# Block-diagonal q half by VectorE copies, residuals in the activation buffers, and a fixed VectorE order through the Out-projection

## The chip, the cores and the metric

The kernel runs on one core of one Trainium2 chip. The metric is the device time of one execution, in microseconds (us); 17 runs of the kernel before have a median of 1339.47 us. TensorE (PE in the profile) multiplies, VectorE (DVE) and ScalarE (ACT) work element by element, SyncE (SP) issues the transfers (DMA), and GpSimd (POOL) does next to nothing here. PEld is TensorE's weight load.

## The reference

Two layers, each an attention and a token-mixing MLP, on x of 2048 x 1024 in bf16. The attention has 32 heads of 32 columns; a position looks at eight positions, itself and every second one before it. The MLP mixes the 2048 positions, with 3584 hidden units. Both are added to x.

```python
def _A_ref(x, wqkv, wo):
    H = 32; Dh = D // H
    W, dil = 8, 2
    q, k, v = ...
    off = jnp.arange(W) * dil
    idx = pos[:, None] - off[None, :]
    logits = einsum("bhsd,bhswd->bhsw", q, kg) * Dh ** -0.5
    attn = softmax(where(idx >= 0, logits, -1e9))
    o = einsum("bhsw,bhswd->bhsd", attn, vg)
    return o.reshape(B, S, D) @ wo

def _B_ref(x, w1, b1, w2, b2):
    u = gelu(einsum("bsd,sf->bdf", layernorm(x), w1) + b1)
    return (einsum("bdf,fs->bds", u, w2) + b2).transpose(0, 2, 1)

x = x + _A_ref(layernorm(x), A_wqkv, A_wo)
x = x + _B_ref(layernorm(x), B_w1, B_b1, B_w2, B_b2)
x = x + _A_ref(layernorm(x), A_wqkv, A_wo)
x = x + _B_ref(layernorm(x), B_w1, B_b1, B_w2, B_b2)
```

## The kernel before, in words

The positions are split by their residue c modulo 2, which makes the dilated window a plain window of eight neighbours. A tile (c, i) is 128 such positions; there are 16. `order` lists them, c = 0 first.

A layer starts with the normalised x, transposed (`hT`), and the value projection. Then come 16 **units**: unit u is one group g of four heads (128 columns) and one residue c. A unit has two **visits** (b = 0, 1), each for four tiles. In a visit TensorE runs, in a fixed order (`in_order`): the scores of (u, b); the values of the visit before; two chunks of the q/k projection of the unit after (`qk_chunk`; visit 0 does the two halves of q, visit 1 those of k), eight matmuls each.

- `scores` (line 372) multiplies blocks of 32 keys with `qB`, in which q stands block-diagonally: head h fills partitions 32h to 32h+31 of column block h, all else is zero. So one matmul gives the scores of four heads. The last matmul of visit 0 reaches eight columns into the second half of q. ScalarE then takes the exponential (`pc`, line 384), and VectorE multiplies four pieces of 32 partitions with the band mask into `Pm` (line 389).
- `qk_chunk` (line 348): for q, ScalarE casts the product to `qs` (pool `qsp`, two buffers, line 360), and four transfers bring the heads' rows to their places in `qB` (line 363), all issued by SP, in order (`chain_("SP", ...)`). Two halves of four heads make eight transfers for a unit. For k a cast into `kT` is enough (line 357).
- `values` (line 393) multiplies `Pm` with the values and with ones into one accumulator `acc` (a single buffer); ScalarE turns the sums into reciprocals `rd` (lines 425 and 426), and VectorE multiplies them into `oT` (line 428), which frees `acc`.

In the last unit there is no next projection. Instead the two visits run the Out-projection of tiles (0, 0) to (0, 3), and the other twelve tiles follow. `out_proj` (line 447) does two halves of 512 columns, eight matmuls each (line 456). VectorE adds the residual `xr` to each (line 458, result `xn`), `xn` is stored, and the normalisation for the MLP follows at once: two statistics (line 181), their aggregate (183), two small ScalarE steps (175, 176), a small VectorE step (193), and ScalarE's activation into `h2` (194). `xr`, `xn` and `rd` share the six buffers of the pool `x2p`; two residuals are loaded ahead. The products use two `m` buffers, so that a half can start only when the add of the half before the last is done.

The MLP follows: `gemm1` (its first block takes the tiles of `h2` one after the other, line 488) and `gemm2` (line 531), whose tiles VectorE adds to the residual (line 534) and SP stores. The pool `gop` has 14 buffers. They hold the activations `g` in the MLP; in the attention eight of them hold `oT`, and six are free.

The order of work on VectorE, ScalarE and SP is set when the program is built, by a scheduler that keeps what `in_order` and `chain_` fix and puts the rest where it can go.

Of the kernel before, what the change touches and what calls it, by code (L numbers as in the profile page):

```python
# [9 lines left out]
ACT = mybir.ActivationFunctionType  # L10
# [4 lines left out]
P = 128  # L15
# [3 lines left out]
DIL = 2  # L19
# [6 lines left out]
def kernel(  # L26
# [42 lines left out]
    def pool(name, bufs, **kw):  # L69
        return ctx.enter_context(tc.tile_pool(name=name, bufs=bufs, **kw))  # L70
# [8 lines left out]
    pcp = pool("pcp", 2)  # L79
    qsp = pool("qsp", 2)  # L80
    dram = pool("dram", 1, space=bass.MemoryType.DRAM)
# [266 lines left out]
    def qk_chunk(u, wts, part, n):  # L348
        g, c = divmod(u, DIL)
        ps = m_tile()  # L350
        lo = c * SC + n * 512
        for kt in range(KD):
            mm = nc.tensor.matmul(ps[:], lhsT=wts[part][:, kt, (g % 2) * P:(g % 2 + 1) * P], rhs=hT[:, kt, lo:lo + 512],  # L353
                                  start=(kt == 0), stop=(kt == KD - 1))
        ls = slice(n * 512, (n + 1) * 512)
        if part:
            nc.scalar.copy(out=kT[u % 2][:, ls], in_=ps[:])  # L357
        else:
            qs = qsp.tile([P, 512], BF16, name="qs", tag="qs")
            nc.scalar.copy(out=qs[:], in_=ps[:])  # L360
            for h in range(HG):
                hp = slice(h * DH, (h + 1) * DH)
                chain_("SP", lambda: nc.sync.dma_start(out=qB[u % 2][hp, h, ls], in_=qs[hp, :]))  # L363
        return mm
# [7 lines left out]
    def scores(u, b):  # L372
# [3 lines left out]
        for i in range(HB):  # L376
            lo = (b * HB + i) * P
            for r in range(P // KG):
# [6 lines left out]
                             func=ACT.Exp, scale=scale, bias=shift[:])  # L385
        for r in range(P // KG):
            rp = slice(r * KG, (r + 1) * KG)
            mk = band[rp].unsqueeze(1).unsqueeze(1).to_broadcast([KG, HB, HG, GW])
            nc.vector.tensor_tensor(out=Pm[rp, :, s0:s0 + HB, r * KG:r * KG + GW].rearrange("p h t k -> p t h k"),  # L389
                                    in0=pc[rp], in1=mk, op=ALU.mult)  # L390
        return mm

    def values(u, b, v, oT):
# [33 lines left out]
        lo = c * SC + t0 * P  # L427
        nc.vector.tensor_tensor(out=oT[g][:, lo:lo + HB * P], in0=acc[:, 0, :], in1=rd[:], op=ALU.mult)
        return mm

    def load_wo(tiles):
# [10 lines left out]
    def load_xr(res):  # L442
        t = x2("xr")
        xrs.append(t)
        chain_("SP", lambda: nc.sync.dma_start(out=t[:], in_=res(*todo.pop(0))))

    def out_proj(c, i, oT, wo, res, dst, h2):
        xr = xrs.pop(0)
        if todo:
            load_xr(res)  # L450
        xn = x2("xn")
        for n in range(NDC):
            ps = m_tile()
            xs_ = slice(n * 512, (n + 1) * 512)
            for g in range(NG):
                mm = nc.tensor.matmul(ps[:], lhsT=oT[g][:, cols(c, i)], rhs=wo[n][g // 4][:, g % 4, :],  # L456
                                      start=(g == 0), stop=(g == NG - 1))
            nc.vector.tensor_tensor(out=xn[:, xs_], in0=ps[:], in1=xr[:, xs_], op=ALU.add)  # L458
        nc.sync.dma_start(out=rows(dst, c, i), in_=xn[:])
        h2[c][i] = vhp.tile([P, D], BF16, name="h2", tag="vh")  # L460
        mean, rs = stats(xn, 1.0 + EPS, eps2)
        norm_act(h2[c][i][:], xn[:], mean, rs)
        return mm

# [59 lines left out]
    def gemm2(c, i, w2t, g, src, dst, to_hT):  # L524
# [3 lines left out]
        aps, _ = pair(i * DIL + c)  # L528
        for dc in range(NDC):
            for ft in range(FT):  # L530
                nc.tensor.matmul(aps[dc], lhsT=w2t[ft // HF][:, ft % HF, c::DIL],  # L531
                                 rhs=g[ft // GF][:, ft % GF, dc * 512:(dc + 1) * 512],
                                 start=(ft == 0), stop=(ft == FT - 1))
            nc.vector.scalar_tensor_tensor(out=xo[:, dc * 512:(dc + 1) * 512], in0=aps[dc], scalar=b2_sb[:, i, c:c + 1],  # L534
                                           in1=xs[:, dc * 512:(dc + 1) * 512], op0=ALU.add, op1=ALU.add)
        nc.sync.dma_start(out=dst, in_=xo[:])
        if to_hT:
# [5 lines left out]
    for li in range(2):  # L543
# [23 lines left out]
        for part, n in chunks:  # L567
            in_order(qk_chunk, 0, wts, part, n)
        wo = None
        for vis in range(2 * NU):  # L570
# [67 lines left out]
```

## Time and profile before

| | |
|---|---|
| median of 17 runs (lowest, highest) | 1339.47 us (1337.24, 1346.59) |
| the profiled execution, its time | 1339.67 us |
| its span, first to last instruction | 1337.6 us |
| start-up and value projection, layer 1 | to about 65.5 us |
| attention of layer 1, units 0 to 14 | 65.5 to 224.5 us |
| its last unit | 224.5 to 241.2 us |
| the rest of the Out-projection | 241.2 to 284.4 us |
| MLP of layer 1 | 284.4 to 670.9 us |
| value projection of layer 2 | 670.9 to 726 us |
| attention of layer 2, units 0 to 14 | 726 to 887 us |
| last unit and Out-projection of layer 2 | 887 to 946.8 us |
| MLP of layer 2 | 946.8 to 1337.6 us |

The times in rows of the profile are counted from the start of the span. A row of the timeline has start, length, engine, line, operation and, in brackets, how long the engine was idle before and what ended the idling. SPq is SP's queue, in which the issue of one transfer is one entry. A row of the chain of waits has start, length and what the end of the program waited for in that stretch.

### The profile page before, as it was taken

The page shows a single profiled execution, that of the slowest core. Times are in us where ns is not written, and L with a number is a line of the kernel's source. Part 1 is how long each engine was busy: PE and PEld are TensorE (multiplying, and loading weights), DVE is VectorE, ACT ScalarE, POOL GpSimd, SP SyncE. Part 2 cuts the span into 40 slices and gives each one's busy share as a digit, 9 for nine tenths or more (in the row PEclk, how much of TensorE's full clock was granted, in tenths as well). Part 3 has the DMA queues.
Part 4 walks back from the last instruction along what each step waited for, and adds up shares of the span by engine and source line. Part 5 has one row for each costly group of instructions (what it writes and reads, how often), then busy time and mean ns, then how long its engine had stood idle before and what let it go on. Part 6 is the DMA issues. An engine that isn't in the chain of part 4 may idle for free.

```text
span 1337.6 us, 19460 instructions
## 1 busy us (share of the span) xinstructions
PE 1285.1 (96%) x8258; PEld 594.1 (44%) x8414; DVE 384.2 (29%) x715; ACT 376.0 (28%) x628; POOL 2.4 (0%) x15
## 2 busy tenths in 40 slices
PE   9989898999999999999999988999999999999998
PEld 4444444444444444444444443444444444444443
DVE  7435556840000013232300554578300000011111
ACT  5356565541111110000033565655311111000000
POOL 0000000000000000000000000000000000000000
PEclk9999999999999999999999999999999999999999
DMA  8422132752222226455500222227422221334420
GB/s 232 75 60 61 53 92 69 222 164 65 79 79 67 78 74 166 116 154 142 135 24 8 58 60 58 91 88 225 137 79 79 71 81 55 118 93 125 133 89 32
DMA packets 208102, 130.01 MB, mean 97 GB/s; under 512 B 42000, under 2 KB 189712, under 8 KB 208016
## 3 DMA queue, kind: packets, MB, share of 16 engines
q1 hardware_dynamic: 208016, 128.76, 33.7%
q8 instruction: 66, 1.08, 0.3%
q14 instruction: 20, 0.16, 0.0%
HBM read 96.48 MB, written 16.78 MB: 85 GB/s over the span
## 4 chain that ended last, share of the span: by engine, by line
PE 81%; DMA 6%; SPq 5%; ACT 3%; issue 2%; DVE 2%; another core or an unknown queue 0%; ACTq 0%; DVEq 0%
PE s L531 14%; PE s L488 14%; PE acc L488 7%; PE m L488 7%; PE m L531 7%; PE acc L531 7%; PE m L353 7%; PE m L456 6%; SPq L363 4%; DMA qB<-qs 4%; PE m L338 4%; PE m L256 4%; ACT pc L384 1%; DMA wo<-in_A_wo_dram 1%; ACT rd L425 1%
## 5 line engine op out<-in xcount | busy, mean ns | idle before, releaser
L488 PEld LDWEIGHTS <-w 128*128 128x128 bf16 x1792 | 175.3, 98 | 211.4
L531 PEld LDWEIGHTS <-w 128*128 128x128 bf16 x1792 | 175.3, 98 | 211.4
L353 PE MATMUL m<-hT,wqk 128*128 128x512 bf16 x963 | 225.0, 381 | 6.2 <-issue 4.6
L488 PE MATMUL s<-h,w 128*128 128x512 bf16 x878 | 201.2, 379 | 0.8
L531 PE MATMUL s<-g,w 128*128 128x512 bf16 x884 | 199.3, 379 | 0.7
L389 DVE TENSOR_TENSOR Pm<-pc,band 32x640 bf16<-32x640 bf16 x256 | 123.6, 483 | 228.1 <-ACT pc L384 222.2
L534 DVE SCALAR_TENSOR_TENSOR xo<-s,b_sb,xs 128x512 bf16<-128x512 f32 x32 | 24.0, 751 | 540.7 <-PE s L531 538.6
L353 PEld LDWEIGHTS <-wqk 128*128 128x128 bf16 x1024 | 95.6, 98 | 119.2 <-issue 12.9
L456 PE MATMUL m<-wo,oT 128*128 128x512 bf16 x500 | 111.5, 379 | 5.5 <-DVE xn L458 4.7
L488 PE MATMUL acc<-h,w 128*128 128x512 bf16 x440 | 103.1, 379 | 0.5
L531 PE MATMUL acc<-g,w 128*128 128x512 bf16 x436 | 99.6, 379 | 0.5
L488 PE MATMUL m<-h,w 128*128 128x512 bf16 x438 | 98.5, 379 | 0.5
L531 PE MATMUL m<-g,w 128*128 128x512 bf16 x436 | 98.3, 379 | 0.6
L175 ACT ACTIVATE ln<-mv,eps 128x1 f32<-128x1 f32 x64 | 18.9, 295 | 235.3 <-DVE mv L183 229.9
L456 PEld LDWEIGHTS <-oT 128*128 128x128 bf16 x512 | 49.6, 98 | 66.0 <-issue 7.7
L495 ACT ACTIVATE g<-s,b_sb 128x1024 bf16<-128x1024 f32 x28 | 31.2, 1114 | 166.9 <-PE s L488 155.2
L381 PE MATMUL s<-qB,kT 128*32 128x160 bf16 x1024 | 36.7, 235 | 30.1 <-DMA qB<-qs 29.3
L384 ACT ACTIVATE pc<-s,shift 128x640 bf16<-128x640 f32 x64 | 51.0, 797 | 31.3 <-PE s L381 31.3
L256 PE MATMUL m<-wv,hT 128*128 128x512 bf16 x250 | 55.6, 379 | 1.0 <-ACT hT L250 0.7
L338 PE MATMUL m<-wv,hT 128*128 128x512 bf16 x251 | 55.2, 379 | 0.3
L360 ACT CAST qs<-m 128x512 bf16<-128x512 f32 x64 | 37.5, 586 | 53.5 <-PE m L353 49.7
L357 ACT CAST kT<-m 128x512 bf16<-128x512 f32 x64 | 37.5, 586 | 46.3 <-PE m L353 46.3
(56 smaller groups left out, 656.6 us busy)
## 6 DMA issues: line engine op xcount, KB each, us to landing
w<-in_B_w_dram SPq DMA_DIRECT2D x56, 512.0 KB, 3.7
w<-in_B_w_dram SPq DMA_DIRECT2D x64, 448.0 KB, 4.6
wqk<-in_A_wqkv_dram SPq DMA_DIRECT2D x16, 512.0 KB, 5.0
qB<-qs SPq DMA_DIRECT2D x256, 32.0 KB, 1.9
xa<-xn SPq DMA_DIRECT2D x32, 256.0 KB, 2.4
xs<-xa SPq DMA_DIRECT2D x32, 256.0 KB, 3.2
wv<-in_A_wqkv_dram SPq DMA_DIRECT2D x8, 512.0 KB, 5.4
wo<-in_A_wo_dram SPq DMA_DIRECT2D x8, 512.0 KB, 6.6
```

The costliest lines, as they stand in the source:

```text
L256: r = nc.tensor.matmul(pss_[k, n][:], lhsT=hT[:, kt, cols(*order[k])], rhs=wv[n][kt // 4][:, kt % 4, :], start=(kt == 0), stop=(kt == KD - 1))
L338: nc.tensor.matmul(ps[:], lhsT=hT[:, kt, cols(c, i)], rhs=wv[n][kt // 4][:, kt % 4, :], start=(kt == 0), stop=(kt == KD - 1))
L353: mm = nc.tensor.matmul(ps[:], lhsT=wts[part][:, kt, (g % 2) * P:(g % 2 + 1) * P], rhs=hT[:, kt, lo:lo + 512], start=(kt == 0), stop=(kt = ...
L357: nc.scalar.copy(out=kT[u % 2][:, ls], in_=ps[:])
L360: nc.scalar.copy(out=qs[:], in_=ps[:])
L363: chain_("SP", lambda: nc.sync.dma_start(out=qB[u % 2][hp, h, ls], in_=qs[hp, :]))
L381: mm = nc.tensor.matmul(dst, lhsT=k[:, lo + r * KG:lo + (r + 1) * KG], rhs=q[:, :, lo + r * KG:lo + r * KG + GW], start=True, stop=True)
L384: nc.scalar.activation(out=pc[:].rearrange("p (n t) h k -> p n (t h k)", n=2), in_=ss[:, :, 0:2 * HG * GW], func=ACT.Exp, scale=scale, bia ...
L389: nc.vector.tensor_tensor(out=Pm[rp, :, s0:s0 + HB, r * KG:r * KG + GW].rearrange("p h t k -> p t h k"), in0=pc[rp], in1=mk, op=ALU.mult)
L456: mm = nc.tensor.matmul(ps[:], lhsT=oT[g][:, cols(c, i)], rhs=wo[n][g // 4][:, g % 4, :], start=(g == 0), stop=(g == NG - 1))
L488: nc.tensor.matmul(pairs[fl][0][dc], lhsT=wt[c][:, i, fl * P:(fl + 1) * P], rhs=h2[c][i][:, dc * 512:(dc + 1) * 512], start=(k == 0), stop ...
L531: nc.tensor.matmul(aps[dc], lhsT=w2t[ft // HF][:, ft % HF, c::DIL], rhs=g[ft // GF][:, ft % GF, dc * 512:(dc + 1) * 512], start=(ft == 0), ...
```

## The change

1. Block-diagonal q: from unit 1 on, heads 0 and 1 are copied into `qB` by VectorE, heads 2 and 3 by transfers as before; in unit 0 VectorE copies all four. `qs` moves from its pool of two buffers to the free buffers of `gop`; `qsp` is gone.
2. The residuals `xr` also move to `gop`, and three instead of two are loaded ahead.
3. In the last unit the order of VectorE is written out: two of the four masks, the multiply into `oT`, the add of a half, then the other two masks or a step of a normalisation.
4. In the whole Out-projection VectorE takes one half of a tile, then a step of an earlier tile's normalisation (`ln_step`: first statistic; second statistic, aggregate and the ScalarE steps; the small step and the activation). The normalisations lag behind the adds by two to three tiles. The first w1 loads are issued six tiles later (k = 8, 10 instead of 2, 4).
5. The last tile of the last `gemm2` is computed in parts of 512, 384 and 128 columns, each stored by itself.

```diff
-    qsp = pool("qsp", 2)
...
-            qs = qsp.tile([P, 512], BF16, name="qs", tag="qs")
+            qs = gop.tile([P, 512], BF16, name="qs", tag="go")
             nc.scalar.copy(out=qs[:], in_=ps[:])
             for h in range(HG):
                 hp = slice(h * DH, (h + 1) * DH)
-                chain_("SP", lambda: nc.sync.dma_start(out=qB[u % 2][hp, h, ls], in_=qs[hp, :]))
+                if h < HG // 2 or u == 0:
+                    nc.vector.tensor_copy(out=qB[u % 2][hp, h, ls], in_=qs[hp, :])
+                else:
+                    chain_("SP", lambda: nc.sync.dma_start(out=qB[u % 2][hp, h, ls], in_=qs[hp, :]))
...
-        t = x2("xr")
+        t = gop.tile([P, D], BF16, name="xr", tag="go")
...
+    def ln_step():
+        if late:
+            late.pop()()
+        if lns:
+            parts = lns[0]
+            parts.pop(0)()
+            if len(parts) == 1:
+                late.append(lns.pop(0)[0])
...
-                load_xr(res)
-                load_xr(res)
+                for _ in range(3):
+                    load_xr(res)
             in_order(scores, u, b)
+            if u + 1 < NU:
+                mask(0, 1, 2, 3)
+            else:
+                chain_("DVE", mask, 0, 1)
             if vis:
                 in_order(values, *divmod(vis - 1, 2), v, oT)
+                if u + 1 < NU:
+                    norm.pop()()
+                else:
+                    chain_("DVE", norm.pop())
             for n in range(2):
                 if u + 1 < NU:
                     in_order(qk_chunk, u + 1, wts, *chunks[2 * b + n])
+                    continue
+                half, add, store, ln = out_proj(0, 2 * b + n, oT, wo, res, xa[li], h2)
+                in_order(half, 0)
+                chain_("DVE", add, 0)
+                if n == 0:
+                    chain_("DVE", mask, 2, 3)
                 else:
-                    in_order(out_proj, 0, 2 * b + n, oT, wo, res, xa[li], h2)
+                    ln_step()
+                in_order(half, 1)
+                chain_("DVE", add, 1)
+                store()
+                lns.append(list(ln))
+                if n:
+                    ln_step()
         in_order(values, NU - 1, 1, v, oT)
         for k, (c, i) in enumerate(order[4:]):
-            if k in (2, 4):
-                chain_("SP", load_w1, k // 2 - 1)
-            out_proj(c, i, oT, wo, res, xa[li], h2)
+            if k in (8, 10):
+                chain_("SP", load_w1, k // 2 - 4)
+            half, add, store, ln = out_proj(c, i, oT, wo, res, xa[li], h2)
+            for n in range(2):
+                half(n)
+                chain_("DVE", add, n)
+                ln_step()
+                if norm:
+                    chain_("DVE", norm.pop())
+            store()
+            lns.append(list(ln))
+        while lns or late:
+            ln_step()
...
+        if final:
+            parts[1:] = [(512, 384, aps[1][:, 0:384]), (896, 128, s_tile()[:, 0, 0:128])]
```

TensorE's order of instructions stays the same up to the last tile. The following rows are instructions in the order in which an engine gets them (line, operation, result<-inputs, shape, and how many alike follow each other; numbers behind names tell buffers apart).

SP at the start of layer 1's attention, before the change: the q transfers of units 0, 1 and 2 (qB_122 is the even units' buffer, qB_123 that of the odd ones), with weight loads between.

```order
L345 DMA wqk<-in_A_wqkv_dram 128x8x256 x2
L363 DMA qB_122<-qs 32x512 x8
L363 DMA qB_123<-qs 32x512 x8
L345 DMA wqk<-in_A_wqkv_dram 128x8x256 x2
L363 DMA qB_122<-qs 32x512 x8
```

And SP at the same place after it (qB_119 is the even units' buffer, qB_120 the odd ones'):

```order
L344 DMA wqk<-in_A_wqkv_dram 128x8x256 x2
L365 DMA qB_120<-qs 32x512 x4
L344 DMA wqk<-in_A_wqkv_dram 128x8x256 x2
L365 DMA qB_119<-qs 32x512 x4
L365 DMA qB_120<-qs 32x512 x4
```

Unit 0 has no q transfer any more, every other unit has four instead of eight, and the weight loads keep their places between the units.

VectorE in an inner unit before the change, from the masks of a visit 0 on; the two multiplies into oT belong to the unit before and to this one:

```order
L389 TENSOR_TENSOR Pm<-pc,band 32x4x4x40 x4
L428 TENSOR_TENSOR oT<-acc,rd 128x512
L389 TENSOR_TENSOR Pm<-pc,band 32x4x4x40 x4
L428 TENSOR_TENSOR oT<-acc,rd 128x512
L389 TENSOR_TENSOR Pm<-pc,band 32x4x4x40 x4
```

And after it:

```order
L398 TENSOR_TENSOR Pm<-pc,band 32x4x4x40 x4
L437 TENSOR_TENSOR oT<-acc,rd 128x512
L363 COPY qB_120<-qs 32x512 x4
L398 TENSOR_TENSOR Pm<-pc,band 32x4x4x40 x4
L437 TENSOR_TENSOR oT<-acc,rd 128x512
```

The four copies for the next unit's q stand behind the multiply into oT of visit 0 and ahead of the masks of visit 1.

VectorE in the last unit before the change, from the masks of its first visit on:

```order
L389 TENSOR_TENSOR Pm<-pc,band 32x4x4x40 x4
L428 TENSOR_TENSOR oT<-acc,rd 128x512
L458 TENSOR_TENSOR xn<-m,xr 128x512
L181 BN_STATS bn<-xn 128x6
L458 TENSOR_TENSOR xn<-m,xr 128x512
L181 BN_STATS bn<-xn 128x6
L183 BN_AGGR mv<-bn 128x2
L458 TENSOR_TENSOR xn<-m,xr 128x512
```

And after it:

```order
L398 TENSOR_TENSOR Pm<-pc,band 32x4x4x40 x2
L437 TENSOR_TENSOR oT<-acc,rd 128x512
L474 TENSOR_TENSOR xn<-m,xr 128x512
L398 TENSOR_TENSOR Pm<-pc,band 32x4x4x40 x2
L474 TENSOR_TENSOR xn<-m,xr 128x512 x2
L485 BN_STATS bn<-xn 128x6
L474 TENSOR_TENSOR xn<-m,xr 128x512
```

The first add now stands behind two masks instead of four, the other two masks behind it, and the first statistic behind three adds instead of one. At the second visit the same happens with the masks and the first add there.

More of the change, by code (lines that the diff above doesn't have):

```diff
@@ L385, in scores, with mask @@
                              func=ACT.Exp, scale=scale, bias=shift[:])
-        for r in range(P // KG):
+        exps[:] = pc, s0
+        return mm
+    exps = []
+    def mask(*rs):
+        pc, s0 = exps
+        for r in rs:
             rp = slice(r * KG, (r + 1) * KG)
             mk = band[rp].unsqueeze(1).unsqueeze(1).to_broadcast([KG, HB, HG, GW])
-            nc.vector.tensor_tensor(out=Pm[rp, :, s0:s0 + HB, r * KG:r * KG + GW].rearrange("p h t k -> p t h k"),
+            mm = nc.vector.tensor_tensor(out=Pm[rp, :, s0:s0 + HB, r * KG:r * KG + GW].rearrange("p h t k -> p t h k"),
                                     in0=pc[rp], in1=mk, op=ALU.mult)
@@ L427, in values @@
         lo = c * SC + t0 * P
-        nc.vector.tensor_tensor(out=oT[g][:, lo:lo + HB * P], in0=acc[:, 0, :], in1=rd[:], op=ALU.mult)
+        norm.append(lambda: nc.vector.tensor_tensor(out=oT[g][:, lo:lo + HB * P], in0=acc[:, 0, :], in1=rd[:], op=ALU.mult))
         return mm
+    norm = []
     def load_wo(tiles):
@@ L451, in out_proj, with half @@
         xn = x2("xn")
-        for n in range(NDC):
+        def half(n):
             ps = m_tile()
-            xs_ = slice(n * 512, (n + 1) * 512)
             for g in range(NG):
@@ L568 @@
             in_order(qk_chunk, 0, wts, part, n)
-        wo = None
         for vis in range(2 * NU):
```

55 lines of the change are left out of this document (43 added, 12 removed).

## The prediction

> **What bounds the kernel now.** I read the page's first part, then TensorE's waits, then the busy time by stage, then the chain of work around one wait.
>
> ```profile
> span 1337.6 us, 19460 instructions
> PE 1285.1 (96%) x8258; PEld 594.1 (44%) x8414; DVE 384.2 (29%) x715; ACT 376.0 (28%) x628; POOL 2.4 (0%) x15
> ```
>
> TensorE is busy for 96% of the span. VectorE and ScalarE are busy for under a third each, so what the change can win is TensorE's idle 52.5 us. The waits view says who ends it (sum in us, times, longest):
>
> ```profile
> PE s L381 <- DMA qB<-qs: 29.3, 32, 2.0
> PE m L456 <- DVE xn L458: 4.7, 6, 1.6
> PE m L353 <- issue: 4.6, 29, 0.2
> ```
>
> The 32 waits of line 381 are about one for each of 16 units in two layers: the scores of a unit wait for the block-diagonal q to be copied by transfers. Both attention stages show it in their busy time (columns: length, TensorE busy, weight loads, VectorE, ScalarE, POOL, granted clock, DMA):
>
> ```profile
> 65.50:224.50 159.00, 141.05 (x1781) 68.81 (x1808) 77.99 (x149) 93.17 (x154) 0.00 (x0) 1.00 0.22 62
> 726.00:887.00 161.00, 142.57 (x1779) 69.17 (x1808) 77.98 (x149) 93.07 (x154) 0.00 (x0) 0.99 0.22 61
> ```
>
> About 18 us are idle in each. A unit's chain shows which link is late; first two rows of the timeline (start, length, engine), then four of the chain that ended last (start, length, what):
>
> ```profile
> 106.42 0.59 ACT L360 CAST qs<-m 128x512 bf16<-128x512 f32 x1 [0.38 <-PE m L353]
> 108.15 0.59 ACT L360 CAST qs<-m 128x512 bf16<-128x512 f32 x1 [1.14 <-PE m L353]
> ```
>
> ```profile
> 110.13 0.59 SPq L363
> 110.76 0.59 SPq L363
> 111.39 1.88 DMA qB<-qs
> ...
> 113.41 0.18 PE s L381
> ```
>
> The first half of q is there at 107.01, the second at 108.74. SP then issues eight transfers one after the other, 0.63 us apart (110.13 to 110.76): 107.03 + 7 x 0.63 = 111.4, where the eighth starts. It lands 1.88 us later, and the last score matmul starts at 113.41. The late link is the queue of eight issues, not the landing of one transfer.
>
> **Term 1: the q waits.** From the second unit on, two heads go by VectorE and two by transfers. SP now issues two after each cast: 107.03 and 107.66, then, with the queue empty, 108.76 and 109.39. The last one starts 2.00 us before it did (111.39 - 109.39). The longest of the 32 waits is 2.0 us. If a landing takes as long as it took beside the same loads before, all 32 fall away; in a layer's first unit no q transfer is left. **-29.3 us.**
>
> **Term 2: the restart.** A stalled visit and the only one without a stall can be laid side by side:
>
> ```profile
> 112.45 0.46 PE L381 MATMUL s<-qB,kT 128*32 128x160 bf16 x15
> 113.41 0.23 PE L381 MATMUL s<-qB,kT 128*32 128x160 bf16 x1 [0.50 <-DMA qB<-qs]
> 114.29 3.40 PE L353 MATMUL m<-hT,wqk 128*128 128x512 bf16 x15 [0.16 <-issue]
> ...
> 837.57 0.56 PE L381 MATMUL s<-qB,kT 128*32 128x160 bf16 x16
> 838.78 1.46 PE L353 MATMUL m<-hT,wqk 128*128 128x512 bf16 x6 [0.16 <-issue]
> ```
>
> From the first score to the next projection it is 1.84 us with the stall and 1.21 without: 0.63, of which 0.50 is counted as idle. So each stall costs 0.13 more, some 30 times: **-4.0 us**. The 0.16 before line 353 stands in both visits, so the 4.6 us of "issue" stay.
>
> **Term 3: one slow spell.** The longest wait is followed by matmuls at half the granted clock (0.57 in the window row):
>
> ```profile
> 827.26 0.23 PE L381 MATMUL s<-qB,kT 128*32 128x160 bf16 x1 [2.02 <-DMA qB<-qs]
> 828.14 5.09 PE L353 MATMUL m<-hT,wqk 128*128 128x512 bf16 x15 [0.16 <-issue]
> 828.00:832.00 4.00, 3.86 (x11) 1.41 (x13) 0.57 0.49 130
> ```
>
> Fifteen such matmuls took 5.09 us here and 3.40 in the visit above. I take the spell to follow from the 2.02 us of idle time: **-1.7 us**. The Trainium skill ("TensorE: Matmul & The Clock Gate", section "What's actually happening") puts the fall to half clock after an idle window of about 3.4 us. This wait was shorter; by that rule the spell would have another cause and might stay, and the sum would be 1.7 us smaller. I follow the rows, since the clock fell right behind the wait; the rule is kept as a rival.
>
> **What the VectorE copies cost.** Per unit four copies (eight in a layer's first) of 32x512 stand between the oT multiply of the visit before and the masks. Before, VectorE did this there:
>
> ```profile
> 106.98 0.69 DVE L428 TENSOR_TENSOR oT<-acc,rd 128x512 bf16<-128x512 f32 x1
> ...
> 109.46 2.03 DVE L389 TENSOR_TENSOR Pm<-pc,band 32x640 bf16<-32x640 bf16 x4 [1.79 <-ACT pc L384]
> ...
> 111.52 0.69 DVE L428 TENSOR_TENSOR oT<-acc,rd 128x512 bf16<-128x512 f32 x1
> ```
>
> VectorE waits 1.79 us there for the exponentials, and that is the cover. Behind the copies are queued the masks and the next oT multiply, which frees the one accumulator that the value matmuls need. Without the stall these start at 112.78 (112.45 + 0.33). Masks and multiply take 2.75 (109.46 to 112.21), so the copies must be done by 110.0. Two can run from 107.67, two from the second cast, 108.76: the limit is (110.0 - 107.67)/4 = 0.58 us for a copy. No row shows such a copy. The nearest are these, with one operand, two operands, and one element:
>
> ```profile
> L189 DVE TENSOR_SCALAR x<-x,mv,rs 128x512 bf16<-128x512 bf16 x2 | 0.7, 403 | 0.0
> L389 DVE TENSOR_TENSOR Pm<-pc,band 32x640 bf16<-32x640 bf16 x256 | 123.6, 483 | 228.1 <-ACT pc L384 222.2
> L193 DVE TENSOR_SCALAR bi<-mv,rs 128x1 f32<-128x1 f32 x32 | 6.6, 207 | 1.3 <-ACT rs L176 1.2
> ```
>
> Bounds are 0.21 and 0.48 us; I take 0.40, the row of the same length. Both ends are under 0.58, so the cost is **0**. VectorE's load rises from 5.5 to 7.1 us of an 8.95 us unit. ScalarE keeps its order there, and six free activation buffers replace the two for qs, which can only loosen its casts.
>
> **Term 4: the last unit and the Out-projection.**
>
> ```profile
> 225.01 2.03 DVE L389 TENSOR_TENSOR Pm<-pc,band 32x640 bf16<-32x640 bf16 x4 [1.19 <-ACT pc L384]
> ...
> 228.41 3.61 PE L456 MATMUL m<-wo,oT 128*128 128x512 bf16 x16 [0.21 <-DVE xn L458]
> ...
> 237.05 3.61 PE L456 MATMUL m<-wo,oT 128*128 128x512 bf16 x16 [0.62 <-DVE xn L458]
> ...
> 262.74 0.69 DVE L458 TENSOR_TENSOR xn<-m,xr 128x512 bf16<-128x512 f32 x1 [2.40 <-DMA xa<-xn]
> ...
> 263.48 20.88 PE L456 MATMUL m<-wo,oT 128*128 128x512 bf16 x94 [1.39 <-DVE xn L458]
> ```
>
> The first two waits come from adds that stand behind four masks (2.03 us); two of them now stand behind the add, which is 1.0 us earlier and covers 0.21 and 0.62. What is late next is the reciprocal on ScalarE, by 0.15 at most: I leave 0.3 for both layers. The third wait is an x2 buffer that was not free because residuals and outputs shared six; the residuals now lie in the activation buffers, and six outputs alone are enough for a normalisation that lags by two to three tiles. **-4.4 us** (4.7 - 0.3).
>
> The lag itself: after the last add about three normalisations are left. The rows show the first MLP product reading its first tiles and, beside it, the last normalisation of the old order:
>
> ```profile
> 284.20 0.59 PE L488 MATMUL s<-h,w 128*128 128x512 bf16 x2
> ...
> 285.06 0.59 PE L488 MATMUL s<-h,w 128*128 128x512 bf16 x2
> 285.12 0.69 DVE L181 BATCH_NORM_STATS2 bn<-xn 128x6 f32<-128x512 bf16 x1
> ...
> 286.91 1.24 ACT L194 ACTIVATE h<-xn,bi,rs 128x1024 bf16<-128x1024 bf16 x1 [0.28 <-DVE bi L193]
> ```
>
> From its second statistic to the end of its activation that one took 3.03 us, and 3.75 with its first statistic. Three without any overlap, behind the add, are 0.7 + 3.0 + 2 x 3.75 = 11.2 us. The product takes a tile each 0.86 us (284.20 to 285.06) and reaches the sixteenth at 15 x 0.86 = 12.9: hidden, with 1.7 us to spare; without that cover it costs its excess. The w1 loads are issued six tiles (about 21 us) later and still 20 us before use.
>
> **Term 5: the end.** The last 512 columns are split into 384 and 128.
>
> ```profile
> 6.67 0.61 PE L245 MATMUL s<-ident,x 128*128 128x128 bf16 x8
> ...
> 1333.89 0.75 DVE L534 SCALAR_TENSOR_TENSOR xo<-m,b_sb,xs 128x512 bf16<-128x512 f32 x1 [5.29 <-PE m L531]
> ...
> out_dram<-xo SPq DMA_DIRECT2D x16, 256.0 KB, 2.1
> ```
>
> Eight 128-column matmuls with their loads take 0.61 us, so 28 narrow ones cost TensorE no more than their quarter. The last add is between 0.21 and 0.75 us, in proportion 0.34 (-0.4); a small transfer lands in 1.88, not 2.1. I take **-0.5 us**, between 0 and -0.8.
>
> **Sum.** 29.3 + 4.0 + 1.7 + 4.4 + 0.5 = 39.9. The span goes from 1337.6 to 1297.7. The profiled execution took 1339.67, 2.07 more than its span: 1299.8. It stands 0.2 above the median of the 17 runs, so I say 1299.6.
>
> **Rivals.**
> *The transfers stay late.* Weight loads (three wqk and one wo in a layer) now run into fewer, earlier q transfers. The last landing has 109.39 + 1.88 + 0.14 = 111.41 against 112.7, so 1.3 us of slack. A landing of 5.6 us was the worst of the 256; it would leave 2.4 us in each of eight units: 19 us, 1319; half of them, 1309. Against it: the loads move 2 us forward along with the transfers. Chance 0.10.
> *Slower: the copies hold the masks up.* Above 0.58 us each copy adds four times its excess to some 30 units. The 39.9 us are lost at 0.58 + 39.9/120 = 0.91 us; at 1.0 the time would be 1339.5 + 0.09 x 120 = 1350. For it: the copies read 32 partitions only and no row shows one. Against it: the mask row, also on 32 partitions and with two operands, has 0.48. Chance 0.02, with 0.01 for a copy near 0.91, no change, and 0.04 for one of 0.6 to 0.8, 1302 to 1326, still faster.
> *The half clock stays* (the skill's rule): 1301.3, chance 0.08.
> *The edit misses its aim*, the last score then waiting for something else as late as the transfers were: 1299.6 + 29.3 + 4.0 = 1333; nothing in the timeline is that late, 0.03.
>
> **How the numbers follow.** The forecast has 0.72, with 1296 to 1304 as its own range (the end's bounds, 0.3 in the last unit, what the runs scatter). Going up to 1310 takes in the half clock and the milder late transfers; down to 1294, for restarts at the Out-projection waits that I left out. Measurement tells 0.2%, 2.7 us, from no change. Faster 0.97, same 0.01, slower 0.02.
>
> **What would show it.** The wait of the scores for qB is gone or under 3 us in sum; the attention stages shrink to about 142 and 143 us; a unit lasts 8.95 us, not 9.58; copies last 0.2 to 0.5 us; no spell of half clock; the Out-projection waits under 0.5 us. It is wrong if the scores or values wait for VectorE, or if a transfer beside a weight load still lands late.

## The result and the profile after

The changed kernel takes **1294.78 us** (median of 8 runs, 1293.64 to 1296.46), against 1339.43 us for the kernel before in the same comparison. The ratio is 0.9664, with a 95% interval of 0.9649 to 0.9678: 44.7 us are gone. The prediction was 1299.6 (1294 to 1310); its sign, its mechanism and its range hold, and its sum was 4 to 5 us too small. Executions at a much lower granted clock (1508.13 us of the kernel before, 1683.89 us of the run with the old order) are left out of the times below.

The first part of the page after (busy time of each engine, share of the span, instructions), and the shares of the chain that ended last:

```profile
span 1293.4 us, 19400 instructions
PE 1276.1 (99%) x8286; PEld 593.6 (46%) x8442; DVE 417.2 (32%) x852; ACT 372.8 (29%) x628; POOL 2.4 (0%) x15
...
PE 98%; issue 1%; DVE 0%; DMA 0%; ACT 0%; SPq 0%
```

By these rows TensorE idles 17.3 us instead of 52.5, and its busy time is 9.0 us lower with the same arithmetic: time that a wait or half clock costs can also stand in the lengths of matmuls. VectorE has 33 us more to do and is still busy for a third of the span only. The changed kernel's waits of TensorE (sum in us, times, longest):

```profile
PE m L352 <- issue: 4.6, 29, 0.2
...
PE s L383 <- DMA qB<-qs: 0.4, 1, 0.4
```

Of 32 waits for q one is left; no wait of the Out-projection (line 467 now) for VectorE is. The 4.6 us of "issue" stayed, as the prediction said; the last experiment shows what they are. The busy time of the two attention stages (length, TensorE, weight loads, VectorE, ScalarE, POOL, granted clock, DMA):

```profile
66.10:206.90 140.80, 137.40 (x1780) 67.79 (x1810) 95.93 (x217) 91.81 (x154) 0.00 (x0) 1.00 0.21 58
705.70:847.00 141.30, 137.50 (x1779) 67.77 (x1810) 95.94 (x217) 91.90 (x154) 0.00 (x0) 1.00 0.20 58
```

Some 3.5 us are idle in each, instead of 18. The granted clock is 1.00 in both; the spell of half clock is not there. One unit of the changed kernel in the timeline:

```profile
100.26 3.40 PE L352 MATMUL m<-hT,wqk 128*128 128x512 bf16 x15 [0.16 <-issue]
...
102.63 0.69 DVE L437 TENSOR_TENSOR oT<-acc,rd 128x512 bf16<-128x512 f32 x1
103.23 0.57 DVE L363 COPY qB<-qs 32x512 bf16<-32x512 bf16 x2
...
104.31 0.58 DVE L363 COPY qB<-qs 32x512 bf16<-32x512 bf16 x2 [0.51 <-ACT qs L359]
...
105.01 2.03 DVE L398 TENSOR_TENSOR Pm<-pc,band 32x640 bf16<-32x640 bf16 x4
...
108.00 0.46 PE L383 MATMUL s<-qB,kT 128*32 128x160 bf16 x16
...
109.11 2.11 PE L352 MATMUL m<-hT,wqk 128*128 128x512 bf16 x9 [0.16 <-issue]
```

The four copies (0.28 us each) lie where VectorE used to wait 1.79 us for the exponentials, and the masks start with no wait behind them. The sixteen score matmuls run through in 0.46 us. From projection to projection (100.26 to 109.11) it is 8.85 us; the unit was 9.58 before and predicted at 8.95.

Stage lengths, from the first TensorE row of a stage to that of the next, in us (an attention begins with its first row of the q/k projection, and the stage behind it with the first row of the Out-projection, so that the scores of the last unit count to the attention):

| stage | before | after | difference |
|---|---|---|---|
| start and value projection, layer 1 | 65.8 | 66.1 | +0.3 |
| attention, layer 1 | 159.02 | 140.83 | -18.19 |
| last unit and Out-projection, layer 1 | 59.40 | 56.71 | -2.69 |
| MLP 1 and value projection, layer 2 | 442.02 | 442.02 | 0.00 |
| attention, layer 2 | 161.07 | 141.38 | -19.69 |
| last unit and Out-projection, layer 2 | 59.63 | 56.70 | -2.93 |
| MLP 2 and end | 390.72 | 389.71 | -1.01 |

### The profile page after: what moved, and what is told of

Its sections match the earlier page's. It is cut to its first block, busy times and chain, and to the rows that moved or that the text cites. A ratio compares the mean times of both kernels' runs of the same rounds, so it can differ in the third digit from the quotient of the medians.

```text
span 1293.4 us, 19400 instructions
## 1 busy us (share of the span) xinstructions
PE 1276.1 (99%) x8286; PEld 593.6 (46%) x8442; DVE 417.2 (32%) x852; ACT 372.8 (29%) x628; POOL 2.4 (0%) x15
## 4 chain that ended last, share of the span: by engine, by line
PE 98%; issue 1%; DVE 0%; DMA 0%; ACT 0%; SPq 0%
PE m L352 17%; PE s L594 15%; PE s L547 15%; PE m L467 8%; PE acc L547 7%; PE m L547 7%; PE acc L594 7%; PE m L594 7%; PE m L337 4%; PE m L255 4%; PE s L383 2%; PE acc L418 1%; PE acc L422 1%; PE m L268 0%; DMA qB<-qs 0%
## 5 line engine op out<-in xcount | busy, mean ns | idle before, releaser
L594 PE MATMUL s<-g,w 128*128 128x512 bf16 (+1 forms) x912 | 201.0, 374 | 0.7
L596 DVE SCALAR_TENSOR_TENSOR xo<-s,b_sb,xs 128x512 bf16<-128x512 f32 (+1 forms) x33 | 24.4, 739 | 532.9 <-PE s L594 532.9
L398 DVE TENSOR_TENSOR Pm<-pc,band 32x640 bf16<-32x640 bf16 x256 | 123.6, 483 | 66.0 <-ACT pc L386 56.7
L594 PE MATMUL m<-g,w 128*128 128x512 bf16 (+1 forms) x436 | 96.9, 376 | 0.6
L363 DVE COPY qB<-qs 32x512 bf16<-32x512 bf16 x136 | 38.1, 280 | 90.7 <-ACT qs L359 89.4
```

The lines of the kernel that those rows point to most:

```text
L363: nc.vector.tensor_copy(out=qB[u % 2][hp, h, ls], in_=qs[hp, :])
L398: mm = nc.vector.tensor_tensor(out=Pm[rp, :, s0:s0 + HB, r * KG:r * KG + GW].rearrange("p h t k -> p t h k"), in0=pc[rp], in1=mk, op=ALU.mult)
L594: nc.tensor.matmul(ap, lhsT=w2t[ft // HF][:, ft % HF, c::DIL], rhs=g[ft // GF][:, ft % GF, lo:lo + w], start=(ft == 0), stop=(ft == FT - 1))
```

## The experiments

**Which part brings what.** The theory: the split of q brings nearly all, because eight serial issues were late; the order, the residuals and the end bring some 6 us. Rival: the free activation buffers (qs, xr) help by themselves. First, the changed kernel with no copies:

```diff
-                if h < HG // 2 or u == 0:
+                if False:
```

> The changed kernel with q's four heads by transfers again in every unit (also unit 0), all else as changed; qs has the six activation buffers. Theory (the queue of eight issues on SP holds the last score matmul): the waits for qB return in full, about 28 to 31 us in some 31 waits, the attention stages last 158 to 161 us again, a unit 9.55 to 9.6 us; the time is 1294.8 + 18.2 + 18 to 19.7 = 1331 to 1333. Where a wait reaches about 2 us, line 352's matmuls behind it run at about 427 ns each; where none does, no spell. Rival (the two qs buffers were what held q back): with six buffers the waits stay well under 15 us, the time under 1315.

It took 1334.45 us, 1.5 above the expected 1331 to 1333; ratio to the kernel before 0.9962 (0.9949 to 0.9976). Its waits:

```profile
PE s L383 <- DMA qB<-qs: 31.0, 34, 1.7
```

The waits for q are all back, with qs in six buffers: the rival falls. The attention stages are 160.57 and 158.57 us long, 36.9 more than in the changed kernel, for 30.6 us more of waits (31.0 less the 0.4 left there), 33 in number. So a wait costs 6.3/33 = 0.19 us beyond its idle time.

Then the split alone, in the kernel before (qs in its two buffers, old order, old end):

```diff
-                chain_("SP", lambda: nc.sync.dma_start(out=qB[u % 2][hp, h, ls], in_=qs[hp, :]))
+                if h < HG // 2 or u == 0:
+                    nc.vector.tensor_copy(out=qB[u % 2][hp, h, ls], in_=qs[hp, :])
+                else:
+                    chain_("SP", lambda: nc.sync.dma_start(out=qB[u % 2][hp, h, ls], in_=qs[hp, :]))
```

> The kernel before with the q split alone (heads 0 and 1 and all of unit 0 by VectorE copies); qs keeps its own two buffers, residuals, last unit, Out-projection and end as before. Theory: nearly all of the attention's 37.9 us, so 1339.4 - 37.9 = 1301.5, between 1300.5 and 1304; the waits for qB in sum under 1 us; the Out-projection's 4.7 us of waits stay. Rival (the buffers share in the gain): casts wait for qs, and it stays above 1308.

It took 1301.51 us, ratio 0.9718 (0.9702 to 0.9734), 38.4 below the kernel before on the same chip (1339.89). Its waits:

```profile
PE m L459 <- DVE xn L461: 5.5, 7, 1.8
...
PE s L384 <- DMA qB<-qs: 0.6, 2, 0.4
```

The waits for q are gone, those of the Out-projection all stay. The two edits add up: 38.4 here and 5.4 in the run with all transfers (1339.89 - 1334.45) make 43.8 of the 44.7.

**The Out-projection, cut in two.** The changed kernel with the old order of VectorE and the old normalisation (residuals in `gop`, late w1 loads, split end and split q stay). The loop of the twelve tiles is shown; the last unit goes back to its old form in the same way:

```diff
-            half, add, store, ln = out_proj(c, i, oT, wo, res, xa[li], h2)
-            for n in range(2):
-                half(n)
-                chain_("DVE", add, n)
-                ln_step()
...
-            store()
-            lns.append(list(ln))
+            out_proj(c, i, oT, wo, res, xa[li], h2)
```

> The changed kernel with VectorE's old order in the last unit and the old order of the normalisations (all four masks, then add and the whole normalisation of a tile); q split, residuals in the activation buffers, late w1 loads and the split end stay. Theory of the three waits: the first two of a layer (0.2 and 0.6 us) return, the third does not; 1294.8 + 2 x (0.83 + 0.2 to 0.4) = 1297 to 1297.3. Rival (the lagging normalisations carry the gain): also the third returns, 1300 and above. Rival (the order is worth nothing): 1294.8.

1297.77 us, 0.5 above the expected 1297 to 1297.3; ratio 0.9694 (0.9676 to 0.9711). Its waits:

```profile
PE m L458 <- DVE xn L460: 1.9, 4, 0.6
```

Four short waits are back, two in each layer, and the stage is 58.18 us long in both instead of 56.7: the order is worth 1.5 us a layer. The long third wait stays away. And the residuals alone, in the kernel before, three loaded ahead:

```diff
-        t = x2("xr")
+        t = gop.tile([P, D], BF16, name="xr", tag="go")
```

> The kernel before with the residuals in the activation buffers alone, three loaded ahead. Theory (the third wait was for one of six shared buffers): that wait, 1.4 us in layer 1 and about 1.6 in layer 2, goes, the other two of each layer and all waits for qB stay: 1339.4 - 3.0 - 0.2 to 0.6 = 1335.8 to 1336.3. Rival (the output buffer is late for another reason): 1339.4.

1337.69 us, 2.2 below the kernel before on the same chip; 1335.8 to 1336.3 was expected. The ratio of 0.9987 (0.9973 to 1.0) does not tell it from no change, so the trace has to show it. Its waits:

```profile
PE s L381 <- DMA qB<-qs: 30.6, 34, 1.8
PE m L456 <- DVE xn L458: 1.6, 4, 0.6
```

The long wait of each layer is gone, and nothing else: the stages are 58.08 us, 1.3 and 1.55 less. Layer 2's attention is 159.0 us here, and 161.07 in the profile before; the longest wait for q is 1.8 us instead of 2.02, and there is no spell of half clock.

**Queue of issues, or landing?** In the next run the number of transfers stays eight a unit, but two queues issue them:

```diff
-                if h < HG // 2 or u == 0:
+                if u == 0:
                     nc.vector.tensor_copy(out=qB[u % 2][hp, h, ls], in_=qs[hp, :])
+                elif h < HG // 2:
+                    nc.gpsimd.dma_start(out=qB[u % 2][hp, h, ls], in_=qs[hp, :])
```

> The changed kernel with no copy by VectorE from unit 1 on: heads 0 and 1 are transferred too, but issued by GpSimd's queue, heads 2 and 3 by SP as before. All eight transfers of a unit are there, as in the kernel before, only the queue of issues is split. If the serial issues were what was late, this gives 1294 to 1298 with waits for q under 3 us in sum, provided that GpSimd issues one in no more than about 0.9 us. If the number of transfers in flight or their landing was what was late, the waits stay near 31 us and the time near 1334.

1294.02 us, ratio 0.966 (0.9642 to 0.9679): as fast as the changed kernel. Its waits, and the group of the new issues:

```profile
PE s L385 <- DMA qB<-qs: 0.2, 1, 0.2
```

```profile
L365 POOL DMA_DIRECT2D qB<-qs x120 | 59.2, 497 | 780.1 <-ACT qs L359 706.9 <-DVE Pm L400 72.9 <-issue 0.3
```

With 0.50 us for an issue on the second queue, all eight transfers of a unit, two on each queue behind each cast, are in time. So what was late was the one queue, not the transfers. The VectorE copies are one way to shorten it, not the only one.

With three heads by transfers and one copy (six issues in the one queue):

```diff
-                if h < HG // 2 or u == 0:
+                if h < 1 or u == 0:
```

> The changed kernel with only head 0 copied by VectorE and three heads by transfers. Queue theory: three issues 0.63 us apart after each cast; in the times of the kernel before the last would start at about 110.2 and land at 112.1, with the score matmul ready for it at 112.7. So 1294 to 1298, and waits for q of under 3 us in sum. Rival, that a transfer lands late beside other transfers whatever the queue: more than two transfers each half would bring waits in most units, in proportion a quarter to a half of the 31 us that all four cost: 1303 to 1310.

1299.87 us (1298.76 to 1300.6), ratio 0.9703 (0.9684 to 0.9722): a miss by 2 us, and 3.5 us in waits instead of under 3, on the side of the rival, though short of its 1303 to 1310. The waits, SP's queue and the chain at the longest of them:

```profile
PE s L383 <- DMA qB<-qs: 3.5, 4, 1.2
```

```profile
147.40 3.67 SPq L365 DMA_DIRECT2D qB<-qs  x6
151.11 2.44 SPq L344 DMA_DIRECT2D wqk<-in_A_wqkv_dram  x2
```

```profile
150.48 3.86 DMA qB<-qs
154.34 0.14 issue
```

The sixth transfer starts at 150.48 and lands after 3.86 us instead of the median 1.9. The weight loads are issued 0.6 us behind it, but they are not what the late ones share. The four units that wait so (until 154.48, 164.61, 779.21 and 789.12) have a sixth transfer of 3.86, 3.71, 3.10 and 3.49 us, and only the first has weight loads behind it. All four have a transfer of the queue for instructions inside them. Here is that queue in the DMA view of this run from 160.7 to 164.5, and of the changed kernel from 771.2 to 775.2 (packets, MB, share of 16 engines):

```profile
q8 instruction: 1, 0.02, 2.3%
```

```profile
q8 instruction: 1, 0.02, 2.3%
```

One packet of 16 KB keeps one of the 16 DMA engines for about 1.4 us (2.3% of 16 x 3.8), and the last pieces of q start only when it is through (163.41, after it ended at 163.30). In the changed kernel all 11 q transfers that the trace shows landing after 3 us or more overlap such a packet; one of them is late enough to be waited for (771.21, 3.89 us, the wait of 0.4 above), and no weight load is issued near it. So the rival "the transfers stay late" was real, though by these traces the instructions delay them and not the weight loads beside them; no run takes the instructions away. The 0.63 us that two heads gain over three cover most of it. In the other units six issues are in time, save one that shows as 0.5 us of "issue".

**What a copy may cost.** All four heads by copies (eight copies of about 0.3 us a unit), and then each copy three times over:

```diff
-                if h < HG // 2 or u == 0:
+                if True:
```

> The changed kernel with all four heads of q copied by VectorE in every unit, no q transfer left. The prediction's limit for a copy is (110.0 - 107.67) / 4 = 0.58 us when two copies follow each cast. Eight copies of 0.28 (as the changed kernel's rows have them) are as long as four of 0.56: just under the limit, so the time should stay where the changed kernel's is, 1294 to 1297, and no wait of the scores for q above 0.4 us. If the limit were wrong by 0.1 us (masks later than I think), each of 30 units would lose 0.4 and the time would be about 1307. If the transfers that are left in the changed kernel still cost something, this kernel would be faster than it, by more than 2 us.

```diff
-                    nc.vector.tensor_copy(out=qB[u % 2][hp, h, ls], in_=qs[hp, :])
+                    for _ in range(3 if u else 1):
+                        nc.vector.tensor_copy(out=qB[u % 2][hp, h, ls], in_=qs[hp, :])
```

> The changed kernel with each VectorE copy of q done three times over from unit 1 on: an effective 0.84 us for a copy. The prediction prices an excess over 0.58 us at four copies times 30 units: 4 x 0.26 x 30 = 31 us, so about 1326 (1320 to 1336, as the unit may also lose what its other waits add), with a new wait of the scores or values for VectorE or for what stands behind its masks, about 1 us a unit. Rival: VectorE has room anyhow (a third busy) and the copies are hidden by it: 1295 to 1298. Any single idle time of TensorE of 2 us or more would also show whether half clock follows it; under 1.8 none should.

The first took 1296.61 us, ratio 0.9679 (0.9657 to 0.9701), with no wait for q or VectorE in its list. Its timeline:

```profile
103.68 2.38 DVE L363 COPY qB<-qs 32x512 bf16<-32x512 bf16 x8
...
106.10 2.03 DVE L398 TENSOR_TENSOR Pm<-pc,band 32x640 bf16<-32x640 bf16 x4
...
108.16 0.69 DVE L437 TENSOR_TENSOR oT<-acc,rd 128x512 bf16<-128x512 f32 x1
108.50 0.46 PE L383 MATMUL s<-qB,kT 128*32 128x160 bf16 x16
...
108.90 0.19 PE L414 MATMUL acc<-Pm,v 128*32 128x8 bf16 x4
```

The copies take 2.38 us, the limit was 4 x 0.58 = 2.33; the values start 0.40 us behind the scores instead of 0.29 (108.00 and 108.29 in the changed kernel's timeline). Its two attention stages are 1.0 us longer in sum than those of the changed kernel (283.2 and 282.2). So it stands at the limit, which is confirmed as the place where a cost sets in. The second took 1319.6 us, 6 less than the 1326 expected and just under the range of 1320 to 1336; ratio 0.9851 (0.9832 to 0.9869). Its waits and its timeline:

```profile
PE acc L415 <- DVE oT L438: 19.6, 29, 1.2
```

```profile
101.06 0.46 PE L384 MATMUL s<-qB,kT 128*32 128x160 bf16 x16
...
102.48 1.98 DVE L399 TENSOR_TENSOR Pm<-pc,band 32x640 bf16<-32x640 bf16 x4 [0.38 <-ACT pc L387]
...
102.99 3.40 PE L352 MATMUL m<-hT,wqk 128*128 128x512 bf16 x15 [0.16 <-issue]
...
105.32 3.73 DVE L364 COPY qB<-qs 32x512 bf16<-32x512 bf16 x12
```

The cover has its price, so the rival "hidden anyhow" falls, but the price is lower than I put it: 24.8 us over 30 units is 0.83 a unit, while 3.73 - 2.33 = 1.40 was expected (42 us with the copies as long as they turned out). The rows suggest why. The wait comes behind the scores, so their exponentials go on; the next masks start at 102.48, 0.51 us ahead of the next projection (102.99), where the changed kernel has them 0.31 behind it (100.57 and 100.26). Part of the lateness is made up there. If a unit loses its copies' time less 2.9 us (3.73 - 0.83), an estimate from this one run, the whole gain of the prediction would have been lost at (2.9 + 39.9/30)/4 = 1.06 us a copy, not at 0.91.

**Does idle time of 2 us halve the clock?** More copies of that kind make TensorE idle at will. Four for each copy of the first half of q and five of the second:

```diff
-                    nc.vector.tensor_copy(out=qB[u % 2][hp, h, ls], in_=qs[hp, :])
+                    for _ in range(4 + n if u else 1):
+                        nc.vector.tensor_copy(out=qB[u % 2][hp, h, ls], in_=qs[hp, :])
```

> The changed kernel with each VectorE copy done four times (first half of q) or five times (second half) from unit 1 on, to make TensorE idle for about 2.5 us once in a unit. From the run with three times: a wait sets in that is the time of a unit's copies less 2.91 us (3.73 - 0.82). 18 copies of 0.31 take 5.58, so 2.67 a unit, 30 units: +80, about 1375. Theory of the prediction, that about 2 us of idle time bring a spell of half clock that costs 1.7 us: 30 x 1.7 = 51 more, about 1426, and granted clocks near 0.57 behind each wait. Rival, the rule of an idle window of about 3.4 us in the Trainium skill (TensorE: Matmul & The Clock Gate): no half clock here, 1375.

1405.84 us (two runs, 1402.03 and 1409.64; the first is profiled), ratio 1.0483 (1.0432 to 1.0534), between the two expectations. Two of its 30 waits in the timeline, and the window row behind the first (granted clock is the column ahead of the last two):

```profile
110.90 0.19 PE L415 MATMUL acc<-Pm,v 128*32 128x8 bf16 x4 [2.50 <-DVE oT L438]
...
111.50 5.31 PE L352 MATMUL m<-hT,wqk 128*128 128x512 bf16 x16
...
136.50 0.19 PE L415 MATMUL acc<-Pm,v 128*32 128x8 bf16 x4 [1.80 <-DVE oT L438]
...
137.12 3.63 PE L352 MATMUL m<-hT,wqk 128*128 128x512 bf16 x16
```

```profile
111.50:115.50 4.00, 4.00 (x19) 1.52 (x12) 1.89 (x4) 1.76 (x3) 0.00 (x0) 0.57 0.02 4
```

After 2.50 us the sixteen matmuls take 5.31 us at a granted clock of 0.57, after 1.80 us they take 3.63: 1.7 us, the same price as in the kernel before. Of the 30 waits 19 were of 2.35 to 2.50 us, and 18 of these were followed by slow matmuls; 11 were of 1.80 to 2.23 us, and one of these was (2.19). So 19 spells came, not 30, and the length of the wait alone does not decide: one of 2.19 us brought a spell and one of 2.20 none.

The trace shows what decides. The granted clock changes only at whole multiples of 3.413 us from its first change, and each spell is 3.41 us long. The rows below are stretches on that grid, the second column being TensorE's busy time: ahead of the spell at 111.72; ahead of the one that followed the wait of 2.19 us (849.86 to 852.05); the stretch with most of the wait of 2.20 us that brought none (838.29 to 840.49); the two that share the wait of 2.50 us that brought none (776.13 to 778.63); and, last, the one ahead of the spell in the kernel before, with the wait of 2.02 us:

```profile
108.31:111.72 3.41, 0.91 (x33) 0.49 (x29) 3.32 (x7) 1.08 (x3) 0.00 (x0) 1.00 0.01 2
849.00:852.41 3.41, 1.11 (x41) 0.74 (x44) 3.29 (x8) 1.38 (x2) 0.00 (x0) 1.00 0.00 0
838.76:842.17 3.41, 1.68 (x33) 0.88 (x33) 3.32 (x7) 1.35 (x3) 0.00 (x0) 1.00 0.00 0
773.88:777.29 3.41, 1.97 (x23) 0.74 (x21) 3.16 (x10) 1.63 (x3) 0.00 (x0) 1.00 0.94 268
777.29:780.70 3.41, 2.07 (x35) 1.07 (x35) 3.12 (x8) 1.23 (x2) 0.00 (x0) 1.00 0.16 40
825.18:828.59 3.41, 1.23 (x35) 0.78 (x34) 0.24 (x1) 1.35 (x3) 0.00 (x0) 1.00 0.75 210
```

In all the traces of this case, a stretch at full clock is followed by half clock where TensorE was busy for up to 41% of it (all 50 such stretches), and by full clock from 46% on (all others, some 4900). A wait of 2 us halves the clock when enough of it falls into one stretch, and not when an edge cuts it. The changed kernel has no stretch under 80%. The Trainium skill ("TensorE: Matmul & The Clock Gate", section "What's actually happening") gives half clock after an idle window of about 3.4 us that runs freely. The trace agrees with the window's length; that TensorE must be idle throughout it does not hold here. The same with six copies for each:

> The changed kernel with each VectorE copy done six times from unit 1 on, to make TensorE idle for about 4.4 us once in a unit: 24 copies of 0.31 take 7.44, less 2.91 is 4.53, 30 units: +136, about 1431 at full clock. Both theories on the half clock (about 2 us of idle time, or the Trainium skill's window of about 3.4) expect a spell of it behind each wait, 1.7 us or more each: 1482 or more. If there is no half clock here either, idle time of this length doesn't bring it, and the spell seen in the kernel before has another cause: 1431.

1489.09 us (two runs), ratio 1.1104 (1.1056 to 1.1152). As both theories expected it is over 1482, so its time tells nothing between them. But the idle time came in two pieces, not in one of 4.4 us:

```profile
PE acc L415 <- DVE oT L438: 74.9, 30, 2.5
PE s L384 <- DVE qB L364: 45.6, 30, 2.3
```

No wait was longer than 2.5 us, and half clock came 30 times, so idle time of 3.4 us in one piece is not needed here either.

**The end.** The changed kernel with its last tile undivided:

```diff
-        final = not to_hT and (c, i) == order[-1]
+        final = False
```

> The changed kernel with the last tile undivided as before (two adds and two stores of 512 columns). The stage from the first MLP product of layer 2 to the end was 390.7 us before and is 389.7 in the changed kernel: so +1.0 us, the last stage back at 390.7 and the time about 1295.8. If the gain at the end came from elsewhere (the residuals' or outputs' buffers), the stage stays at 389.7.

1296.27 us, ratio 0.9667 (0.9643 to 0.9692). By the time alone it can't be told from the changed kernel (0.9664); the last stage is 390.73 us long in its profile instead of 389.71, and that is the 1.0 expected. Its trace shows something else. A unit of it, and one row of its first part (busy time, instructions):

```profile
99.73 3.63 PE L352 MATMUL m<-hT,wqk 128*128 128x512 bf16 x16
...
108.58 1.68 PE L352 MATMUL m<-hT,wqk 128*128 128x512 bf16 x7
```

```profile
PE 1286.8 (99%) x8414; PEld 591.7 (46%) x8414; DVE 417.1 (32%) x851; ACT 372.5 (29%) x628; POOL 2.4 (0%) x15
```

The unit lasts 8.85 us as in the changed kernel, but the projection has 16 rows instead of 15 and no 0.16 us of "issue" ahead of it, and there are as many matmuls as weight loads (8414), where the traces of the changed kernel and of the one before lack 156. So the 4.6 us of "issue" are no idle time: the record of each projection's first matmul is missing there. By this fuller trace only 6.5 us (1293.3 - 1286.8) of TensorE's time are idle in this run.

## Why the prediction was right, and where its sizes were off

| term | predicted | measured | from |
|---|---|---|---|
| 1, waits for q | -29.3 | -28.9 | one of 0.4 is left |
| 2, restart | -4.0 | -7.3 | both attention stages lose 37.9; less 28.9 and 1.7 |
| 3, half clock | -1.7 | -1.7 | clock 1.00 in both stages |
| VectorE copies | 0 | 0 | 8.85 us a unit |
| 4, Out-projection | -4.4 | -5.6 | 2.69 + 2.93 |
| 5, end | -0.5 | -1.0 | 390.72 to 389.71 |
| start | 0 | +0.3 | 65.8 to 66.1 |
| sum | -39.9 | -44.2 | span 1337.6 to 1293.4 |

*Term 1* stands with its reason: a second queue alone does the same, and in the split alone the waits are gone with the old buffers.

*Term 2* was mis-sized, and it makes up most of what is missing. The step that failed is the comparison with "the only one without a stall": that visit had its sixteen scores in 0.56 us (837.57), where an undisturbed visit of the changed kernel takes 0.46 (108.00) and reaches the next projection after 1.11 us, not 1.21. The stalled visit, 1.84, then costs 1.84 - 1.11 - 0.50 = 0.23 beyond its idle time and not 0.13, some 31 times: 7.1, against the 7.3 of the stages; the run with all transfers gives 0.19. The 0.23 is also the length of the last score matmul, which runs alone there (113.41, 0.23 in the prediction's rows); when nothing waits it lies among its neighbours, sixteen in 0.46. That this is the cause is not shown by a run of its own.

*Term 3* is supported, with a correction: the spell followed from idle time, but from its share of one stretch of 3.413 us (busy 1.23 of 3.41 us ahead of it), and not from 2.02 us as such. So where a wait falls is luck, and the 1.7 us are those of the one profiled execution. That one spell is typical of the kernel before is not shown: its executions have mean granted clocks between 0.997 and 1.000.

*The copies* took 0.28 us, inside the bounds of 0.21 and 0.48, and the limit of 0.58 was right (eight copies, 2.38 us, stand at it). The price above the limit was too high, as shown; it was needed for a rival only.

*Term 4* was right in its two causes: the order and the residuals' buffers, each tried alone, take away just the waits named. Two sizes were off. The 0.3 us left for the reciprocals is not there: in the last unit the written order leaves TensorE without a wait for VectorE. VectorE's timeline there:

```profile
208.35 0.69 DVE L437 TENSOR_TENSOR oT<-acc,rd 128x512 bf16<-128x512 f32 x1 [0.15 <-ACT rd L435]
208.96 0.68 DVE L474 TENSOR_TENSOR xn<-m,xr 128x512 bf16<-128x512 f32 x1
209.67 1.00 DVE L398 TENSOR_TENSOR Pm<-pc,band 32x640 bf16<-32x640 bf16 x2
```

The reciprocal is late by the 0.15 us named, but by 209.64 the add is done and TensorE is still in the other half. And the stages fell by 0.9 us more than the six waits were long (5.6 - 4.7). The prediction left a restart out there. By the two runs the excess stands at the four short waits (the order is worth 2.95 us for 1.9 us of waits) and not at the two long ones (2.9 us for 3.1), so a restart at each wait is not shown. The lag of the normalisations cost nothing: the stage of MLP 1 is 442.02 us long before and after.

*Term 5*: the last add is 0.35 us (0.34 predicted), but from its end to the end of the span it is 2.3 us now (1291.10 to 1293.4) and was 3.0 (1334.64 to 1337.6). The landing of the smaller store gave 0.7 (1.4 us for the last 32 KB, and 2.0 for 256 KB before), where I had 0.2 at most. The last rows of the timeline:

```profile
1288.98 1.73 PE L594 MATMUL s<-g,w 128*128 128x128 bf16 x28
...
1290.75 0.35 DVE L596 SCALAR_TENSOR_TENSOR xo<-s,b_sb,xs 128x128 bf16<-128x128 f32 x1 [0.95 <-PE s L594]
```

*The rivals.* Late transfers exist, but with two heads in transfers only one of them reaches past the slack, and what delays it is a transfer of instructions, not the weight loads that the prediction named. Copies as a bound need four times 0.58 us, and they take half of that. The half clock did not stay. The edit did not miss its aim.

## What to carry to other kernels

When TensorE waits for a transfer, look first at how many issues stand in one queue ahead of it: here the landing was on time and the eighth place in the queue was late, so moving half of the work to VectorE, or to a second queue, ended the wait. Price a stall by laying the stalled piece beside one that is undisturbed in every row, weight loads included, and count what a wait costs beyond its idle time. What a third engine adds is free up to a limit that can be read from the chain behind it; make the added work longer on purpose to see where the limit lies.

## What the runs showed of the hardware

- TensorE's granted clock changes on a grid of 3.413 us. After a stretch of the grid with TensorE busy for up to 41% (1.4 us of 3.41) the next was at half clock, in 50 of 50 cases; from 46% on it stayed at full clock. A spell costs 1.7 us over sixteen matmuls of 128x512 (5.31 us instead of 3.63). One wait of 2.5 us that an edge of the grid cut (busy 1.97 and 2.07 us) had no spell.
- A wait of TensorE costs some 0.2 us more than its idle time: 6.3 us for 33 waits in the run with all transfers, 7.3 for the 31 waits that the change took away.
- A transfer of 32 KB that has a packet of 16 KB of instructions on one of its DMA engines (about 1.4 us) landed after 3.1 to 3.9 us instead of 1.9 in the five cases where TensorE waited for it.
- GpSimd issued 120 transfers at 0.50 us each, with no harm to the kernel, which it otherwise hardly uses.
